# Moving the output groups of a fused MLP's step behind its third product

## The chip, the cores and the metric

The kernel runs on one core of a Trainium2 chip. The metric is device time in microseconds. Each execution is timed by itself. The profile is one further execution, taken by the hardware profiler.

## What is computed

The program is three layers in a row, all in fp32: an attention with landmarks, a first MLP with a SiLU, and a second, gated MLP, which the change touches. Cut to that one:

```python
def _moe2_ref(x, w_gate, w_val, w_out, rms_g):     # x is 2304 x 512, d_ff 1536
    rms = np.sqrt(np.mean(x * x, axis=-1, keepdims=True) + 1e-06)
    xn = x / rms * rms_g
    g = xn @ w_gate
    silu = g * (1.0 / (1.0 + np.exp(-g)))
    val = xn @ w_val
    return (silu * val @ w_out).astype(np.float32)
```

## The kernel before

The second MLP takes the 2304 tokens in three passes p of two blocks of 384, and the 1536 hidden channels in twelve tiles f of 128. One pair (p, f) is a step, i = 12 p + f, 36 in all, each made by `moe2_step`. A step needs, for each of its two blocks, a 128 x 384 tile of g and one of val. It forms these four products of matrices by a scheme in the manner of Strassen and Winograd: seven products of half depth (k = 0 to 6) with sums of the weights and of x as operands. A product is six matmuls with 384 columns (line 843): two halves of the depth, and each fp32 operand as a pair of a rounded part and its remainder, of which three of the four combinations are taken.

Products are written to two PSUM banks, x and y (one buffer each, `pg`). Product 0 starts bank x; products 2, 3 and 5 add onto it. Product 1 starts bank y; product 4 starts y anew, and product 6 adds onto it. Between two products on a bank its value is read: after product 0 ScalarE copies x to a1, after product 1 VectorE adds y to a1 (g1) and ScalarE takes its SiLU (z1); after product 2 x is copied to u2, after 3 to u3; after 4 v2 = u3 + y on VectorE; after 5 z2 = SiLU(x) on ScalarE; after 6 v1 = u2 + y on VectorE. Then VectorE multiplies z2 by v2 and z1 by v1, and each result is split: a cast on ScalarE (line 146), the remainder on VectorE (line 147). In the rows the step's number and the digits of names are left out: `a<-ga` is a1, `g<-a,gb` is g1, `u<-ga` is u2 or u3, `v<-u,gc` is v1 or v2, `z<-ga` is z2, `u<-z,v` a gated product and `CAST u<-u` its cast. Helpers record these at line 180. `ga` is bank x, `gb` and `gc` are bank y.

The other six PSUM banks hold the output sums of a pass, one for each 128 tokens. The results of a step are multiplied with w_out in the step after it: `out(n)`, n = 0 to 5, calls `out_tile`, three matmuls with 512 columns (line 917). Groups 0 to 2 use the half that is made from z2, groups 3 to 5 the half made from z1 and v1. At the last tile of a pass the group's bank is copied to SBUF and stored. Between the products `moe2_step` also calls `between(k)`, k = 0 to 6, which issues work for later steps: in steps 7 to 10 `late` makes the weight operands of the next step (sums at line 577, splits by `split_w`, stores at lines 589 and 592); in the first two passes a piece of the next pass's norm (`norm_all`: squares, sums, a mean by TensorE at line 773 with its copy at line 774, roots, scaling), and from tile 9 on the splits of the next pass's x (`split_x`, lines 807 and 808). The mean's two results borrow banks x and y. In step 0 two splits of x are left for `between(0)` and `between(2)`.

The order on each engine is fixed when the program is built. The framework tracks what each instruction needs, and of those that are ready by its reckoning it takes for an engine the one that stands earliest in the program; so work that is ready early can stand far ahead of its place in the code. `tc.issue_after(ins)` keeps an instruction behind another: each output group behind the latest product (`mm[0]`), each piece of the norm behind VectorE's and ScalarE's latest. All loads and stores of this part, but for a few of the last outputs, go through SP's queue; the next weights are loaded by `load_split(i + 2)` (line 628) once product 6 has freed their tile, and the output weights by `load_wo2` (line 637).

Of the kernel before, what the change touches and what calls it, by code (L numbers as in the profile page):

```python
# [67 lines left out]
def nystrom_moe_kernel(ctx: ExitStack, tc: tile.TileContext, q, k, v, w_in, w_out, w_gate, w_val, w_out2, rms_g, out):  # L68
# [75 lines left out]
    def split(dst, src, lo=POOL, hi=ACT):  # L144

        x = ACT.copy(dst[:, 0], src) if hi is ACT else hi.tensor_copy(dst[:, 0], src)  # L146
        return x, lo.tensor_tensor(dst[:, 1], src, dst[:, 0].bitcast(F32), op=ALU.subtract)  # L147
# [36 lines left out]
    def finish(gn):  # L184
        for _ in gn:
            pass
# [377 lines left out]
    NI = NB2 // 2 * NF2  # L564

    def load_f32(f):
        fw_t[f] = p2.tile([P, 3 * DM], F32, tag="fw", name=f"fw_{f}", bufs=2)
        SP.dma_start(out=fw_t[f], in_=w2d[f])
# [55 lines left out]
    def load_split(i):  # L624

        if NI > i > 0 and (i >= NF2 or i in PRE):
            w7_t[i] = w7_tile(i, f"w7_{i}")
            SP.dma_start(out=w7_t[i].rearrange("p x n -> p (x n)").bitcast(F32), in_=w7d[i % NF2])
# [4 lines left out]
    def load_wo2(i):  # L633
        if i < NI and (i >= NF2 or i in PRE):
            if i:
                wo2_t[i] = wo2_tile(i)
            SP.dma_start(out=wo2_t[i].rearrange("p x n -> p (x n)").bitcast(F32), in_=wod[i % NF2])

    def late(i, k):

        if PRE_N <= i < NF2:
            if k == 0:
                w7_t[i] = w7_tile(i, f"w7_{i}")
                wo2_t[i] = ps2.tile([P, 2, DM], F32R, tag="oc", name=f"oc_{i}", bufs=3)
            if k < 2:
                sums(i, 2 * k)
                sums(i, 2 * k + 1)
            if k in (0, 1, 3, 4):
                split_w(i, w7_t[i], k - (k > 2))
            if k in (2, 3, 5, 6):  # L650
                store_w(i, w7_t[i], k - 2 - (k > 4))
            if k == 5:
                split(wo2_t[i], fw_t[i][:, 2 * DM:], lo=DVE)
        if PRE_N < i <= NF2 and k == 0:
            store_wo(i - 1, wo2_t[i - 1])
# [142 lines left out]
    def split_x(p, k):  # L798
        j = 7 * (p % 2) + k
        if j < 12:  # L800
            t = (p3x if j < 5 else p3).tile([P, 2, 2, TB], F32R, tag=f"x{j}", name=f"x7_{p}_{k}", bufs=1)
        else:
            t = p2.tile([P, 4 * TB], F32R, tag="fw", name=f"x7_{p}_{k}", bufs=2).rearrange("p (x i t) -> p x i t", x=2, i=2)
        x7[p, k] = t
        c = nx[p][OPS[k]]
        for i in range(2):
            ACT.copy(blocked(t[:, 0, i]), by_landmark(c[:, i]))
            DVE.tensor_tensor(blocked(t[:, 1, i]), by_landmark(c[:, i]), blocked(t[:, 0, i].bitcast(F32)), op=ALU.subtract)
# [17 lines left out]
    def moe2_step(p, f, prev, between):  # L826


        i = p * NF2 + f
        if PRE_N <= i + 2 < NF2:  # L830
            load_f32(i + 2)
        if i:
            load_wo2(i + 1)
        w7 = w7_t[i].rearrange("p x (o k n) -> p x o k n", o=7, k=2)

        def tmp(name):
            return p3t.tile([P, TB], F32, tag=name, name=f"{name}_{i}", bufs=1 if name in ("a1", "g1", "u3", "v2", "z2") else 2)

        def product(k, acc, start, stop):
            o, xs, n = WAT[OPS[k]], x7[p, k], 0  # L840
            for kk in range(2):
                for (x, y) in ((0, 0), (0, 1), (1, 0)):
                    mm[0] = PE.matmul(acc, w7[:, x, o, kk], xs[:, y, kk], start=start and n == 0, stop=stop and n == 5, skip_group_check=True)  # L843
                    n += 1

        def added(name, x, y):
            t = tmp(name)
            VE.tensor_tensor(t, x, y, op=ALU.add)
            return t

        def gated(j, gate, val):
            u = tmp(f"u{j}")
            VE.tensor_tensor(u, gate, val, op=ALU.mult)
            hl = p3t.tile([P, 2, TB], F32R, tag="hl", name=f"u2_{i}_{j}", bufs=4)
            split(hl, u, lo=DVE)
            return hl

        hls, mm = [None, None], [None]

        def out(n):  # L860
            with tc.issue_after(mm[0].ins):
                out_tile(prev, n)

        def copied(name, x):
            t = tmp(name)
            AE.copy(t, x)
            return t

        def silu(name, x):
            t = tmp(name)  # L870
            AE.activation(t, x, AF.Silu)
            return t

        x, y = pg(f"ga_{i}", "x"), pg(f"gb_{i}", "y")
        product(0, x, True, True)
        a1 = copied("a1", x)
        between(0)
        product(1, y, True, True)
        z1 = silu("z1", added("g1", a1, y))
        between(1)  # L880
        out(0)
        product(2, x, False, True)
        u2 = copied("u2", x)
        between(2)
        out(1)
        out(2)
        product(3, x, False, True)
        u3 = copied("u3", x)
        between(3)
        y = pg(f"gc_{i}", "y")  # L890
        product(4, y, True, True)
        v2 = added("v2", u3, y)
        between(4)
        out(3)
        product(5, x, False, True)
        hls[1] = gated(1, silu("z2", x), v2)
        between(5)
        out(4)
        product(6, y, False, True)
        load_split(i + 2)  # L900
        hls[0] = gated(0, z1, added("v1", u2, y))
        between(6)
        out(5)
        return p, f, hls, wo2_t[i]

    oacc = {}
# [1 line left out]
    def out_tile(prev, n):  # L908

        if prev is None:  # L910
            return
        p, f, hls, w = prev
        j, t = 1 - n // 3, n % 3
        if f == 0:
            oacc[n] = po.tile([P, DM], F32, tag="o", name=f"o_{p}_{n}", bufs=6)
        for i, (x, y) in enumerate(((0, 0), (0, 1), (1, 0))):
            PE.matmul(oacc[n], hls[j][:, x, t * P:(t + 1) * P], w[:, y], start=f == 0 and i == 0, stop=f == NF2 - 1 and i == 2)  # L917
        if f == NF2 - 1:
            e = nslot(n, f"e2_{p}_{n}", [P, DM])
            last = 0 if p < NB2 // 2 - 1 else 1 + n // 5  # L920
            if last < 2:
                (DVE.tensor_copy if n % 2 else ACT.copy)(e, oacc[n])
            else:
                DVE.tensor_copy(e[:, :DM // 2], oacc[n][:, :DM // 2])
                ACT.copy(e[:, DM // 2:], oacc[n][:, DM // 2:])
            store_out(e, (2 * p + j) * 12 + t * 4, last)

    def pg(name, tag):
        return pp.tile([P, TB], F32, tag=tag, name=name, bufs=1)
# [169 lines left out]
    for p in range(NB2 // 2):  # L1099
# [3 lines left out]
        def between(k):  # L1103
            if x0 and k in (0, 2):
                split_x(0, x0.pop(0))
            late(p * NF2 + f + 1, k)
            if nxt:
                if 0 < f < NORM_END:
                    next(jobs[0], None)
                elif f:  # L1110
                    if f == NORM_END and k == 0:
                        finish(jobs[0])
                    n = 7 * (f - NORM_END) + k
                    if n in XSPLIT:
                        split_x(nxt, XSPLIT.index(n))
# [17 lines left out]
        for f in range(NF2):  # L1133
            if nxt and f == 1:
                jobs[0] = norm(nxt)
            prev = moe2_step(p, f, prev, between)
# [38 lines left out]
```

## Time and profile before

| | us |
|---|---|
| median of 3 runs | 847.81 (847.7 to 847.9) |
| the profiled execution | 848.19 |
| its span, first to last instruction | 845.2 |
| TensorE busy in it | 827.2 |

The page gives busy times by engine. The view of stretches gives them for parts of the span, with the clock that TensorE was granted as a share of full speed. The view in order of time merges like instructions that follow each other: the start, the time from the first one's start to the last one's end, the engine, the line, what is written and read, the count, and in brackets how long the engine was idle before it and who ended that.

### The profile page before, as it was taken

The page shows a single profiled execution, that of the slowest core. Times are in us where ns is not written, and L with a number is a line of the kernel's source. Part 1 is how long each engine was busy: PE and PEld are TensorE (multiplying, and loading weights), DVE is VectorE, ACT ScalarE, POOL GpSimd, SP SyncE. Part 2 cuts the span into 40 slices and gives each one's busy share as a digit, 9 for nine tenths or more (in the row PEclk, how much of TensorE's full clock was granted, in tenths as well). Part 3 has the DMA queues.
Part 4 walks back from the last instruction along what each step waited for, and adds up shares of the span by engine and source line. Part 5 has one row for each costly group of instructions (what it writes and reads, how often), then busy time and mean ns, then how long its engine had stood idle before and what let it go on. Part 6 is the DMA issues. An engine that isn't in the chain of part 4 may idle for free.

```text
span 845.2 us, 15430 instructions
## 1 busy us (share of the span) xinstructions
PE 827.2 (98%) x5934; PEld 735.3 (87%) x5934; DVE 534.0 (63%) x1185; ACT 446.8 (53%) x919; POOL 20.3 (2%) x47
## 2 busy tenths in 40 slices
PE   6899999999999999999999999999999999999997
PEld 3567787988898989999999999999999999999996
DVE  5879877786579767679844489733558523333333
ACT  2796665676666856676643457533345423223222
POOL 5100000000000000000000000000000000000001
PEclk9899999999999999999999999999999999999999
DMA  9788757368795569998985548667555458555552
GB/s 307 307 286 303 291 169 225 107 205 259 268 332 175 171 205 353 329 362 290 333 296 189 213 174 275 247 237 301 224 220 191 179 202 292 224 214 186 183 200 75
DMA packets 72424, 202.85 MB, mean 240 GB/s; under 512 B 6592, under 2 KB 34240, under 8 KB 68384
## 3 DMA queue, kind: packets, MB, share of 16 engines
q1 hardware_dynamic: 72032, 201.09, 66.8%
q8 instruction: 47, 0.77, 0.4%
q0 software_dynamic: 240, 0.66, 0.3%
q14 instruction: 25, 0.20, 0.1%
q10 hardware_dynamic: 80, 0.13, 0.0%
HBM read 149.29 MB, written 52.56 MB: 239 GB/s over the span
## 4 chain that ended last, share of the span: by engine, by line
PE 95%; DVE 1%; ACT 1%; DMA 1%; issue 0%; SPq 0%; POOL 0%; POOLq 0%
PE a L694 21%; PE ga L843 18%; PE o L917 18%; PE h L674 13%; PE gc L843 9%; PE gb L843 4%; PE a L691 4%; PE pw L502 2%; PE pe L316 1%; DMA kT<-in_k_dram 1%; PE pu L435 1%; PE c L309 1%; PE pq L309 1%; PE ct L418 1%; PE spare L248 1%
## 5 line engine op out<-in xcount | busy, mean ns | idle before, releaser
L694 PE MATMUL a<-hl,wo 128*128 128x288 f32 x1296 | 192.3, 297 | 0.0
L694 PEld LDWEIGHTS a<-hl,wo 128*128 128x128 f32 x1296 | 178.3, 188 | 1.7 <-issue 0.8
L917 PE MATMUL o<-oc,u 128*128 128x512 f32 x648 | 178.9, 394 | 0.0
L843 PE MATMUL ga<-x,w 128*128 128x384 f32 x840 | 171.1, 338 | 0.0
L843 PEld LDWEIGHTS ga<-x,w 128*128 128x128 f32 x840 | 151.3, 188 | 12.4 <-ACT a L180 0.3
L674 PE MATMUL h<-at,wp 128*128 128x288 f32 x768 | 132.5, 307 | 0.0
L917 PEld LDWEIGHTS o<-oc,u 128*128 128x128 f32 x648 | 119.5, 188 | 13.3 <-DVE u L147 0.3
L674 PEld LDWEIGHTS h<-at,wp 128*128 128x128 f32 x768 | 109.6, 189 | 22.6 <-issue 8.6
L180 DVE TENSOR_TENSOR v<-u,gc 128x384 f32<-128x384 f32 x72 | 39.7, 552 | 122.6 <-PE gc L843 122.0
L843 PE MATMUL gc<-x,w 128*128 128x384 f32 x420 | 84.8, 336 | 0.0
L681 ACT ACTIVATE s<-h 128x288 f32<-128x288 f32 x108 | 44.0, 411 | 69.2 <-PE h L674 60.9
L843 PEld LDWEIGHTS gc<-x,w 128*128 128x128 f32 x420 | 75.0, 188 | 2.9
L180 ACT COPY u<-ga 128x384 f32<-128x384 f32 x72 | 34.5, 479 | 71.7 <-PE ga L843 71.4
L146 ACT CAST u<-u 128x384 fp32r<-128x384 f32 x72 | 37.0, 514 | 61.2 <-DVE u L180 61.1
L180 DVE TENSOR_TENSOR u<-z,v 128x384 f32<-128x384 f32 x72 | 40.1, 557 | 46.1 <-ACT z L180 45.1
L147 DVE TENSOR_TENSOR hl<-s,hl 128x288 fp32r<-128x288 f32 x108 | 49.0, 453 | 29.3 <-ACT hl L146 28.7
L147 DVE TENSOR_TENSOR u<-u,u 128x384 fp32r<-128x384 f32 x72 | 40.0, 556 | 26.3 <-ACT u L146 26.0
L180 ACT ACTIVATE z<-ga 128x384 f32<-128x384 f32 x36 | 17.7, 491 | 68.4 <-PE ga L843 68.2
L146 ACT CAST hl<-s 128x288 fp32r<-128x288 f32 x108 | 46.6, 434 | 2.9
L691 PE MATMUL a<-s,wor 128*128 128x288 f32 x160 | 42.9, 407 | 0.0
L843 PE MATMUL gb<-x,w 128*128 128x384 f32 x210 | 42.4, 336 | 0.0
L843 PEld LDWEIGHTS gb<-x,w 128*128 128x128 f32 x210 | 37.0, 188 | 0.2
(167 smaller groups left out, 938.0 us busy)
## 6 DMA issues: line engine op xcount, KB each, us to landing
w<-w7d SPq DMA_DIRECT2D x31, 1792.0 KB, 7.3
oc<-wod SPq DMA_DIRECT2D x32, 512.0 KB, 7.8
win<-wind SPq DMA_DIRECT2D x20, 512.0 KB, 5.5
w2d<-c SPq DMA_DIRECT2D x36, 256.0 KB, 2.5
fw<-w2d SPq DMA_DIRECT2D x12, 768.0 KB, 6.4
winr<-in_moe_w_in_dram SPq DMA_DIRECT2D x8, 1024.0 KB, 8.4
wor<-in_moe_w_out_dram SPq DMA_DIRECT2D x16, 512.0 KB, 7.4
w7d<-w7p SPq DMA_DIRECT2D x16, 512.0 KB, 5.7
```

The source lines that it names most:

```text
L146: x = ACT.copy(dst[:, 0], src) if hi is ACT else hi.tensor_copy(dst[:, 0], src)
L147: return x, lo.tensor_tensor(dst[:, 1], src, dst[:, 0].bitcast(F32), op=ALU.subtract)
L180: self.last = getattr(self.eng, name)(*args, **kw)
L248: PE.matmul(spare[0], mean_w, mean_w.unsqueeze(1).to_broadcast([P, 4, P]), start=True, stop=True)
L309: x = PE.matmul(out[o], lm[y, i, R], t[y, i, lo:hi], start=True, stop=True)
L502: x = PE.matmul(pw[g][32 * i:32 * i + 32], lts[b][hr, i], win_t[i // 2, nb_][hr, i % 2], start=True, stop=True)
L674: PE.matmul(ph, w[:, x, fo:fo + P], a[:, y, tk], start=i == 0, stop=i == 5)
L681: ACT.activation(s, ph, AF.Silu)
L691: PE.matmul(acc[d], w[:, y], hl, start=start, stop=stop)
L694: PE.matmul(acc[d], w[:, x, y], hl[:, z], start=start and i == 0, stop=stop and i == 2)
L843: mm[0] = PE.matmul(acc, w7[:, x, o, kk], xs[:, y, kk], start=start and n == 0, stop=stop and n == 5, skip_group_check=True)
L917: PE.matmul(oacc[n], hls[j][:, x, t * P:(t + 1) * P], w[:, y], start=f == 0 and i == 0, stop=f == NF2 - 1 and i == 2)
```

## The change

The six output groups of a step, which stood in ones and twos behind products 1, 2, 4, 5 and 6, all stand behind product 2. All seven calls of `between` come behind them, where each stood behind its own product. The products then follow as 3, 4, 5, 6 with nothing between them. In the last step of all one group stays behind product 2, and the other five stand behind product 6. No instruction is added or removed.

```diff
         x, y = pg(f"ga_{i}", "x"), pg(f"gb_{i}", "y")
+        late_out = 1 if i == NI - 1 else 6
         product(0, x, True, True)
         a1 = copied("a1", x)
-        between(0)
         product(1, y, True, True)
         z1 = silu("z1", added("g1", a1, y))
-        between(1)
-        out(0)
         product(2, x, False, True)
         u2 = copied("u2", x)
-        between(2)
-        out(1)
-        out(2)
+        for n in range(late_out):
+            out(n)
+        for k in range(7):
+            between(k)
         product(3, x, False, True)
         u3 = copied("u3", x)
-        between(3)
         y = pg(f"gc_{i}", "y")
         product(4, y, True, True)
         v2 = added("v2", u3, y)
-        between(4)
-        out(3)
         product(5, x, False, True)
         hls[1] = gated(1, silu("z2", x), v2)
-        between(5)
-        out(4)
         product(6, y, False, True)
         load_split(i + 2)
         hls[0] = gated(0, z1, added("v1", u2, y))
-        between(6)
-        out(5)
+        for n in range(late_out, 6):
+            out(n)
         return p, f, hls, wo2_t[i]
```

## Rows read from the trace of the kernel before

**Rows 1.** The page, busy time by engine: us, share of the span, instructions.

```profile
PE 827.2 (98%) x5934; PEld 735.3 (87%) x5934; DVE 534.0 (63%) x1185; ACT 446.8 (53%) x919; POOL 20.3 (2%) x47
```

**Rows 2.** Stretches: length, busy time of each engine, TensorE's granted clock, DMA.

```profile
480.00:520.00 40.00, 40.00 (x209) 37.02 (x208) 31.60 (x62) 24.41 (x46) 0.00 (x0) 1.00 0.57 206
...
720.00:760.00 40.00, 40.00 (x210) 37.24 (x209) 13.35 (x25) 12.06 (x25) 0.00 (x0) 1.00 0.59 225
```

**Rows 3.** In order of time, TensorE in the last step but one.

```profile
812.03 1.20 PE L843 MATMUL ga<-x,w 128*128 128x384 f32 x6
...
814.81 1.22 PE L843 MATMUL ga<-x,w 128*128 128x384 f32 x6
815.87 1.55 PE L917 MATMUL o<-oc,u 128*128 128x512 f32 x6
...
821.81 1.22 PE L843 MATMUL gc<-x,w 128*128 128x384 f32 x6
822.87 0.86 PE L917 MATMUL o<-oc,u 128*128 128x512 f32 x3
823.56 1.21 PE L843 MATMUL ga<-x,w 128*128 128x384 f32 x6
```

**Rows 4.** In order of time, step 0 and the start of step 1.

```profile
422.90 1.20 PE L843 MATMUL ga<-x,w7p 128*128 128x384 f32 x6
...
423.94 0.88 PE L843 MATMUL gc<-x,w7p 128*128 128x384 f32 x4
...
426.05 0.48 ACT L180 COPY u<-ga 128x384 f32<-128x384 f32 x1 [0.41 <-PE ga L843]
...
426.58 1.33 PE L843 MATMUL ga<-x,w7p 128*128 128x384 f32 x6 [0.22 <-ACT u L180]
427.75 1.22 PE L843 MATMUL gc<-x,w7p 128*128 128x384 f32 x6
...
428.81 1.21 PE L843 MATMUL ga<-x,w 128*128 128x384 f32 x6
...
429.01 0.56 DVE L180 TENSOR_TENSOR v<-u,gc 128x384 f32<-128x384 f32 x1
...
429.86 1.20 PE L843 MATMUL gb<-x,w 128*128 128x384 f32 x6
...
430.11 0.48 ACT L180 COPY a<-ga 128x384 f32<-128x384 f32 x1 [0.53 <-PE ga L843]
430.68 0.51 ACT L146 CAST u<-u 128x384 fp32r<-128x384 f32 x1
```

**Rows 5.** In order of time, the mean in bank x, from step 4 into 5.

```profile
472.75 0.49 ACT L180 ACTIVATE z<-ga 128x384 f32<-128x384 f32 x1 [2.32 <-PE ga L843]
...
473.95 0.56 DVE L774 COPY rv<-pm 128x384 f32<-128x384 f32 x1
...
475.51 0.34 PE L843 MATMUL ga<-x,w 128*128 128x384 f32 x1
```

**Rows 6.** In order of time, the start of step 8.

```profile
510.56 1.21 PE L843 MATMUL ga<-x,w 128*128 128x384 f32 x6
...
511.36 1.14 ACT L146 CAST w<-t 128x512 fp32r<-128x512 f32 x2
...
512.81 0.47 ACT L180 COPY a<-ga 128x384 f32<-128x384 f32 x1
...
513.35 1.32 PE L843 MATMUL ga<-x,w 128*128 128x384 f32 x6
```

**Rows 7.** In order of time, ScalarE at the start of the last step.

```profile
824.69 0.51 ACT L146 CAST u<-u 128x384 fp32r<-128x384 f32 x1 [1.68 <-DVE u L180]
825.11 0.47 ACT L180 COPY a<-ga 128x384 f32<-128x384 f32 x1
```

**Rows 8.** In order of time, TensorE's weight loads at the end.

```profile
837.90 1.22 PEld L917 LDWEIGHTS o<-oc,u 128*128 128x128 f32 x6 [0.29 <-DVE u L147]
```

**Rows 9.** DMA issues: what, queue, operation, count, size, median us to landing.

```profile
w<-w7d SPq DMA_DIRECT2D x31, 1792.0 KB, 7.3
```

## The prediction

> **What bounds the kernel now.** The first thing read is the page's busy times: TensorE works in 98% of the span [rows 1]. The second is the table of stretches inside the second MLP, where the change lies: TensorE is busy for all of each stretch at a granted clock of 1.00, while VectorE is busy 31.6 of 40 us in one stretch and 13.4 in another [rows 2]. So this part is bound by TensorE's own columns, and an edit that adds and removes no matmul can gain only what lies between matmuls, and can lose wherever it takes work away from behind which another engine now hides.
>
> The third view is one quiet step in order of time [rows 3]. From one first product to the next it takes 823.56 - 812.03 = 11.53 us. Products 2 and 6 hold TensorE for 1.06 us (814.81 to 815.87, 821.81 to 822.87), an output group for 0.69 (822.87 to 823.56). Seven products and six groups give about 7 x 1.05 + 6 x 0.69 = 11.5, so nothing is idle. The fourth is step 0 with the start of step 1 [rows 4], which has no output groups before it, since there is no previous step: it shows what the products do when they stand directly behind each other, as the change wants them.
>
> **The change, part by part.** Its diff moves output groups and filler work only. Products alternate between two PSUM banks, x (products 0, 2, 3, 5) and y (1, 4, 6). Between two products on a bank an engine has to read it. I call this a turn.
>
> *What a turn needs.* A product's six matmuls show as 1.22 us, but the next product starts 1.05 later, so the last one drains for about 0.17. Product 6 ends at 427.75 + 1.22 = 428.97 and the add that reads it starts at 429.01: 0.04. The add takes 0.56. A ScalarE copy takes 0.48; the one at 426.05 ends at 426.53, and the product that waits for it shows at 426.58, 0.05 later, and lasts 1.33 in place of 1.22, so 0.11 of weight load is uncovered [rows 4]. From a product's end to the next use of its bank this makes 0.04 + 0.48 + 0.05 + 0.11 = 0.68 us behind ScalarE and 0.76 behind VectorE. One product in between gives 1.05 - 0.17 = 0.88. So a turn with a single product in it still has 0.20 to spare with ScalarE and 0.12 with VectorE. Step 0 agrees: product 6 runs at 427.75, product 0 at 428.81 and product 1 at 429.86 without a gap.
>
> *What is taken away.* Today the turns hold, beside a product, one or two output groups of 0.69. After the change the six groups (4.1 us) all lie in the turn of product 2 to 3. Five turns of a step are left with one product: a1 (product 0 to 2), u3 (3 to 5), v2 (4 to 6), z2 (5 to the next 0), v1 (6 to the next 1). The groups' own inputs do not get late: the halves of the previous step are ready before its next product 2 ends, since the cast of the second one stands at 430.68 [rows 4] and the fourth group starts 2.1 us behind the run's start. In a quiet step all five turns fit, so they cost 0; the bounds are 0 and, with 0.1 missing in each, 0.5 a step.
>
> *What may come back.* A product that follows an output group takes 1.06, product 2 of step 0, which follows a product, 1.04 (422.90 to 423.94); products 5 and 6 of step 0 are no cleaner (product 6 takes 427.75 to 428.81, 1.06). Three products a step lose such a neighbour. At best that is 3 x 0.02 x 35 = 2.1 us; I take the one that is clean in step 0 [rows 4], 0.02 x 35 = 0.7, and keep 0 and 2.1.
>
> *The mean of the norm.* In steps 4 and 16 two matmuls of the mean borrow bank x and two bank y (line 773). The pair on x waits for z2, and the next step's product 0 waits for its copy. Today product 6 and an output group lie in between: z2 starts at 472.75, the copy ends at 473.95 + 0.56 = 474.51, product 0 comes at 475.51 [rows 5]. Without that group it would come at 474.81. From z2's start to the copy's end are 1.76 us; with 0.09 ahead (0.04, and the 0.05 of the weight load's signal) and 0.16 behind that is 2.0 after product 5's end, against 1.05 + 0.35 - 0.17 = 1.23 of matmuls: 0.8 uncovered. The pair on y now comes before product 4 is written and is hidden by product 3, which gives back about 0.3. So +0.5 in each of two steps, +1.0; bounds 0 and +1.6.
>
> *The fillers.* The weight splits of late (steps 7 to 10) and the splits of x for the next pass move behind the run. In the program they now stand before products 3 to 6, but each engine's order is fixed by readiness, and they can go ahead of a1 and v1 as soon as their slot is free. The trace shows this today in step 8 [rows 6]: two weight casts, 1.14 together, stand before a1, which could start at 510.56 + 1.21 + 0.04 = 511.81 and starts at 512.81. Product 2 behind it takes 1.32 in place of 1.22, 0.1 lost although a group of 0.69 still lay in the turn. With the group gone the same delay would cost 0.8. But the order is made anew, so I take one cast in front of a1 in each of four steps, 0.57 - 0.20 = 0.37, in all 1.5; and a VectorE subtraction of the add's shape in front of v1 or v2 in three turns, 3 x (0.56 - 0.12) = 1.3. Sum 2.8. The lower bound is 0 (all of it finds its place in the 4.1 us of groups, where both engines have little else to do), the upper one such delay in all five turns of seven busy steps, 7 x 5 x 0.44 = 15.
>
> *Edges and queues.* The last step keeps one group behind product 2 and has five behind product 6: the 0.29 wait near the end [rows 8] goes, of which TensorE's next matmul feels perhaps 0.2; product 3 there has 0.69 - 0.17 = 0.52 for a turn of 0.68, which costs 0.16. Net 0. The load of the next weights (lines 626 to 628) is still issued behind product 6, but the product that needs it comes one group, 0.7, sooner: 11.5 us against 7.3 to landing [rows 9]; hidden, and 0 too. The stores of late now precede that load on SP's queue; they are ready several products earlier, so they hold nothing up. The evictions of steps 12 and 24 fall into the run, where nothing waits for them within a step.
>
> **Sum.** -0.7 + 1.0 + 2.8 + 0 = +3.1 us. The profiled execution took 848.19, 0.38 over the median of 847.81, so the sum is put on the median: about 850.8.
>
> **The rivals.**
> *No difference.* The fillers fit into the run and cost nothing. Then -0.7 + 1.0 = +0.3: 848.1. For it speaks that VectorE has room even in the busy stretch [rows 2]; against it the start of step 8 [rows 6], where casts go far ahead of their place.
>
> *Faster.* Fillers cost 0, and all three products recover 0.02: -2.1 + 0.5 gives 846.2, and with the mean hidden too 845.7. It decides from the point where the turns cost less than 0.4 in all. Against it speaks product 6 of step 0.
>
> *The wrong order on ScalarE.* In quiet steps today the cast of u stands before a1 (824.69, then 825.11 [rows 7]). If that order stayed, a1 would have to wait for v1 (0.04 + 0.56), the product u of the same shape (0.56, and 0.04 to start), the cast's share of 0.42, then 0.48 + 0.16: 2.26 after product 6's end, where product 2 wants 2 x 1.05 - 0.17 = 1.93. That loses 0.3 in each of 34 steps, 10 to 11: 858. Against it: in step 1, where no group lies behind product 6, a1 already goes first (430.11, cast 430.68). The Trainium skill, Perfetto Trace Analysis, section Optimizing Tensor Performance, asks that independent groups of matmuls rotate through different PSUM banks so that reading one out overlaps the next group. It speaks against this change, which runs seven products over two banks where output groups on six others used to lie between; step 0 [rows 4] shows two banks sufficing as long as nothing stands in front of the reader.
>
> **How the numbers follow.** A run tells about 0.2%, 1.7 us, from no change. Forecast (fillers delay a few turns, 849 to 854) 0.48; no difference 0.28; faster 0.12; wrong order or every busy turn paying 0.12. The forecast's low edge adds 0.04 to the middle. So faster 0.12, same 0.32, slower 0.56. The range goes from 846.2 to 857.0: it takes in the faster case's better half and most of the busy-turn bound, and leaves out the full 15.
>
> **What would show it.** Right: quiet steps still at 11.5 us; the idle time of TensorE before products 2, 1 and 6 named after ScalarE's copy and VectorE's adds, in steps 7 to 10 and around 20 only; steps 4 and 16 longer by half a microsecond. Wrong: quiet steps that are longer (the third rival), or shorter than 11.48 (the second), or steps 7 to 10 without idle time (the first).

## The result and the profile after

The changed kernel takes 853.2 us (median of 4 runs, 853.0 to 853.7) against 847.85 (847.7 to 847.9) for the kernel before: ratio 1.0064, 95% interval 1.005 to 1.0078, so it is slower by 5.35 us. The forecast was slower, 850.8, with a range of 846.2 to 857.0. The profiled execution took 853.25, with a span of 850.8 against 845.2.

The page's busy times by engine:

```profile
PE 830.1 (98%) x5934; PEld 733.5 (86%) x5934; DVE 531.7 (62%) x1185; ACT 446.0 (52%) x919; POOL 20.3 (2%) x47
```

The two stretches, with the columns of [rows 2]:

```profile
480.00:520.00 40.00, 39.31 (x197) 34.75 (x196) 29.80 (x58) 23.51 (x45) 0.00 (x0) 1.00 0.57 209
720.00:760.00 40.00, 40.00 (x211) 37.42 (x210) 11.86 (x23) 11.12 (x23) 0.00 (x0) 1.00 0.58 215
```

TensorE's busy time is 2.9 us above that of [rows 1] for the same 5934 matmuls, and its share is the same: this row doesn't tell where the time went. In the busy stretch it was full before and now has 0.69 us idle, and VectorE gets through less work in the same 40 us (29.80 against 31.60). The quiet stretch is as full as it was. The clock stands at 1.00 in both, so it is no part of the story.

A quiet step in order of time, TensorE and one add of VectorE (the counterpart of [rows 3]; output groups are now line 911):

```profile
819.57 1.20 PE L843 MATMUL ga<-x,w 128*128 128x384 f32 x6
820.61 4.34 PE L911 MATMUL o<-oc,u 128*128 128x512 f32 x18
824.79 1.23 PE L843 MATMUL ga<-x,w 128*128 128x384 f32 x6
825.86 1.20 PE L843 MATMUL gc<-x,w 128*128 128x384 f32 x6
826.90 1.22 PE L843 MATMUL ga<-x,w 128*128 128x384 f32 x6
827.16 0.56 DVE L180 TENSOR_TENSOR v<-u,gc 128x384 f32<-128x384 f32 x1 [6.18 <-PE gc L843]
827.96 1.22 PE L843 MATMUL gc<-x,w 128*128 128x384 f32 x6
829.01 1.20 PE L843 MATMUL ga<-x,w 128*128 128x384 f32 x6
...
831.10 1.20 PE L843 MATMUL ga<-x,w 128*128 128x384 f32 x6
```

From one product 2 to the next (819.57 to 831.10) are 11.53 us, exactly as before, with the eighteen matmuls of the groups in one run and seven products back to back. So the loss is not spread over the steps. The table gives the length of each kind of step, from the start of one product 1 to the start of the next, in the two profiles; steps 5 and 6, and 17 and 18, are taken together, since TensorE's order crosses their border.

| | before | after | difference |
|---|---|---|---|
| first product starts at | 420.82 | 421.10 | +0.28 |
| steps 4 and 16 (mean of the norm) | 12.48, 12.53 | 12.97, 13.05 | +1.01 |
| 5 with 6, 17 with 18 | 23.14, 23.18 | 24.41, 24.35 | +2.44 |
| steps 7, 8, 9 | 34.70 | 35.69 | +0.99 |
| steps 19, 20, 21 | 34.71 | 34.96 | +0.25 |
| steps 1, 14, 25 | 34.63 | 35.20 | +0.57 |
| the other 20 whole steps | 11.53 to 11.58, step 0 7.99 | within 0.02 each | -0.1 |
| last step from product 1 on | 20.61 | 20.73 | +0.12 |

Together +5.56, against 5.57 between the spans. What TensorE's weight loads waited for in the second MLP (the four largest; us in total, times, longest) says who is late:

```profile
PEld gb L843 <- DVE v L180: 2.1, 3, 1.0
PEld ga L843 <- ACT u L180: 1.5, 5, 0.5
PEld ga L843 <- DVE rv L774: 1.2, 2, 0.6
PEld ga L843 <- ACT a L180: 1.2, 4, 0.4
```

The third line is the mean. The first, with a wait of 1.0, is the largest, and nothing in the prediction has that size. It lies at the end of step 5. TensorE, ScalarE and VectorE there, in order of time:

```profile
480.06 4.34 PE L911 MATMUL o<-oc,u 128*128 128x512 f32 x18
...
481.12 1.28 ACT L780 ACT_TABLE_LOAD   x1
482.42 0.94 ACT L780 ACTIVATE rv<-rv,eps 128x768 f32<-128x768 f32 x1
...
486.35 1.22 PE L843 MATMUL ga<-x,w 128*128 128x384 f32 x6
...
487.65 1.28 ACT L180 ACT_TABLE_LOAD   x1 [1.61 <-PE ga L843]
...
488.67 0.55 DVE L180 TENSOR_TENSOR v<-u,gc 128x384 f32<-128x384 f32 x1 [1.49 <-PE gc L843]
488.95 0.49 ACT L180 ACTIVATE z<-ga 128x384 f32<-128x384 f32 x1
...
489.27 0.62 PE L843 MATMUL gb<-x,w 128*128 128x384 f32 x2 [0.65 <-DVE v L180]
...
489.73 1.20 PE L843 MATMUL ga<-x,w 128*128 128x384 f32 x6
```

The norm's square root (line 780) is one of the things that `between` issues. With the fillers it moved into the run of groups, where its own table load costs nothing. But the next SiLU (z2, behind product 5) needs its own table back. That load stands right ahead of z2 and, though its row names nothing that it reads, starts only when product 5 is done (486.35 + 1.22 = 487.57): in ScalarE's order the semaphore wait for product 5, which ends at 487.62, stands ahead of the load. So z2 starts at 488.95 instead of about 487.67. Product 0 of the next step, which needs bank x from z2, comes at 489.73; at a quiet step's pace it would have come two products, 2.11, behind product 5, at 488.46. That is 1.27 us. The wait row names v1, since TensorE's order has two matmuls of product 1 ahead of product 0 here; but v1 is prompt (488.67, against product 6's end at 487.41 + 1.22 = 488.63), and it is z2 that product 0 needs. Before, the same two loads stood thus:

```profile
483.00 1.28 ACT L780 ACT_TABLE_LOAD   x1
...
483.99 1.22 PE L843 MATMUL ga<-x,w 128*128 128x384 f32 x6
...
484.30 0.94 ACT L780 ACTIVATE rv<-rv,eps 128x768 f32<-128x768 f32 x1
...
485.05 0.86 PE L917 MATMUL o<-oc,u 128*128 128x512 f32 x3
...
485.29 1.28 ACT L180 ACT_TABLE_LOAD   x1
...
486.59 0.49 ACT L180 ACTIVATE z<-ga 128x384 f32<-128x384 f32 x1
...
486.80 0.86 PE L917 MATMUL o<-oc,u 128*128 128x512 f32 x3
...
487.50 1.21 PE L843 MATMUL ga<-x,w 128*128 128x384 f32 x6
```

z2 was as late behind its product as now (486.59 against the product's end at 485.21, 1.38; after, 488.95 against 487.57), but two output groups of 0.69 lay in that turn, and TensorE felt at most the 0.08 by which step 5 (11.61) was longer than a quiet one. The table load is not new. Its cover went.

### The profile page after: what moved, and what is told of

Same layout as the page of the kernel before. It is cut to its first block, busy times and chain, and to the rows that moved or that the text cites. A ratio compares the mean times of both kernels' runs of the same rounds, so it can differ in the third digit from the quotient of the medians.

```text
span 850.8 us, 15382 instructions
## 1 busy us (share of the span) xinstructions
PE 830.1 (98%) x5934; PEld 733.5 (86%) x5934; DVE 531.7 (62%) x1185; ACT 446.0 (52%) x919; POOL 20.3 (2%) x47
## 4 chain that ended last, share of the span: by engine, by line
PE 90%; ACT 4%; DMA 3%; DVE 2%; issue 1%; SPq 0%; ACTq 0%
PE ga L843 18%; PE a L694 18%; PE o L911 18%; PE h L674 11%; PE gc L843 9%; PE gb L843 5%; PE a L691 4%; PE pw L502 2%; PE pe L316 1%; DMA r_g<-in_moe_w_gate_dram 1%; DMA kT<-in_k_dram 1%; PE pu L435 1%; PE c L309 1%; DMA w7d<-w7p 1%; PE pq L309 1%
## 5 line engine op out<-in xcount | busy, mean ns | idle before, releaser
L911 PE MATMUL o<-oc,u 128*128 128x512 f32 x648 | 156.4, 394 | 0.0
L843 PEld LDWEIGHTS ga<-x,w 128*128 128x128 f32 x840 | 148.7, 188 | 6.3 <-DVE rv L774 1.2
L911 PEld LDWEIGHTS o<-oc,u 128*128 128x128 f32 x648 | 121.5, 188 | 25.5
```

## The experiments

**Which part of the move costs: the groups or the fillers.** First the run of groups alone, with each filler left behind its own product (against the changed kernel):

```diff
         product(0, x, True, True)
         a1 = copied("a1", x)
+        between(0)
         product(1, y, True, True)
         z1 = silu("z1", added("g1", a1, y))
+        between(1)
...
         for n in range(late_out):
             out(n)
-        for k in range(7):
-            between(k)
+        between(2)
```

and so on for 3 to 6.

> Only the output groups are moved; the seven calls of between stand behind their own products again. Theory (the loss lies in other engines' work that falls into turns with one product): the pieces of the norm now fall right into these turns, a square root with its table loads behind u3 among them, so it is slower than the changed kernel, 854 to 858 us, with long waits in steps 5 and 17 and more of them in steps 6 to 8 and 18 to 20. Rival (the loss comes from the moved fillers, not from the groups): 848 to 849 us.

Measured: 856.2 (855.96 to 856.85), ratio to the kernel before 1.01 (1.0085 to 1.0114): 3 us worse than the change as it is. Steps 4 and 16 grow to 14.2 each, 2.4 of the 3; steps 7 to 9 do not get longer (35.44). So taking the fillers into the run does pay, and above all in the two steps of the mean.

Then the reverse, the fillers behind product 2 and the groups at their old places:

```diff
+        out(0)
         product(2, x, False, True)
         u2 = copied("u2", x)
-        for n in range(late_out):
-            out(n)
+        out(1)
+        out(2)
         for k in range(7):
             between(k)
...
         u3 = copied("u3", x)
...
+        out(3)
```

with groups 4 and 5 behind products 5 and 6.

> Only the calls of between are moved behind product 2; the output groups stand where they stood before. Theory: every turn keeps its 0.69 or more of groups, so the square root, the table loads and the casts are hidden as before: 847.3 to 848.6 us, no difference. Rival (the moved fillers are what costs): 851 to 853 us.

Measured: 847.12, ratio 0.999 (0.9982 to 0.9999). Moving the fillers alone costs nothing; the 0.08 to 0.11 that steps 5 and 8 had lost before are gone (11.53 each). The whole loss needs the groups out of the turns.

**The table of the SiLU.** If the reload ahead of z2 is the cause, it must vanish when something calls for that table at once, while the run of groups covers the load. A SiLU of one column, whose result nobody uses, follows the square root:

```diff
+    touch = cst.tile([P, 9], F32, name="touch")[:, 0:1]
...
+        if p:
+            ACT.activation(touch, rv[:, 1, TB - 1:], AF.Silu)
```

> The changed kernel with one more ScalarE instruction behind the norm's square root: a SiLU of one column, whose result is not used, so that the table of the SiLU comes back while the output groups run. Theory: product 0 behind steps 5 and 17 waits for z2 because of a table load of 1.28 us in front of it; both steps get shorter by about 1.2, the time falls by 2.4 us to about 850.8. Rival (VectorE's reciprocals hold up v1 and v2 in these steps): no fall, 853.

Measured: 847.4 (846.2 to 849.6), ratio 0.9993 (0.9985 to 1.0002). Steps 5 with 6 fell to 22.86, but the time fell by more than expected, since the quiet steps fell too, to 11.43 to 11.46, and they hold no square root. The new tile of nine columns moves the tiles allocated behind it. So the experiment was made anew with nothing moved: the result goes to a column of a tile that was there already and was unused.

```diff
-    eps = cst.tile([P, 9], F32, name="eps")[:, 0:1]
+    eps9 = cst.tile([P, 9], F32, name="eps")
+    eps, touch = eps9[:, 0:1], eps9[:, 8:9]
...
+        if p:
+            ACT.activation(touch, rv[:, 1, TB - 1:], AF.Silu)
```

> The changed kernel with the SiLU of one column behind the square root, written into a column that the kernel before already holds unused, so that nothing moves in SBUF. Theory: quiet steps stay at 11.53, steps 5 and 6 together fall from 24.4 to 23.1 us, as do 17 and 18: 850.7. Rival (all that the first form of this won was the place of the tiles): 853.2.

Measured: 850.06 (849.4 to 850.6), ratio 1.0025 (1.0015 to 1.0035). ScalarE in step 5, in order of time:

```profile
480.95 1.28 ACT L781 ACT_TABLE_LOAD   x1
482.25 0.94 ACT L781 ACTIVATE rv<-rv,eps 128x768 f32<-128x768 f32 x1
483.20 1.28 ACT L783 ACT_TABLE_LOAD   x1
...
487.44 0.49 ACT L181 ACTIVATE z<-ga 128x384 f32<-128x384 f32 x1 [1.62 <-PE ga L846]
```

The reload stands in the run and z2 has none ahead of it. Steps 5 with 6 take 23.06 and 17 with 18 take 23.14, no more than before the change; the quiet steps stay at 11.53. That is 2.56 us less in these four steps, of the 3.1 by which the time fell; the rest lies in steps 7 and 25 (0.3 together) and in the last step.

The Trainium skill, ScalarE: Activation LUTs, section What ACT_TABLE_LOAD costs, gives 1283 ns for the load and 1380 ns of draining for every switch. The rows agree with the first and not with the second: the SiLU of z2 starts 0.02 us behind its load's end, and the load 0.05 behind the square root's end in the kernel before.

**The place of the tiles.** To see what a moved tile does by itself, the same nine unused columns were put into the kernel before, and into the changed kernel:

```diff
     eps = cst.tile([P, 9], F32, name="eps")[:, 0:1]
+    pad = cst.tile([P, 9], F32, name="pad")[:, 0:1]
+    POOL.memset(pad, 0.0)
```

The kernel before with it:

> The kernel before with one small tile more (nine columns, of which one is set to 0 and none is read), which moves every later tile in SBUF; no instruction of the step changes. Theory (the hundredths that separate 1.04 from 1.06 us of a product hang on where the operands lie, as the SiLU of one column suggested, whose own tile moved them too): quiet steps of 11.41 to 11.46 in place of 11.53 to 11.57, 35 x 0.1 = 3.5 us less, 844 to 845. Rival (they come from output groups next to products): quiet steps as before, 847.9.

The changed kernel with it:

> The changed kernel with the same unused tile. Theory: quiet steps of 11.41 to 11.46, the waits of steps 4 to 8 and 16 to 20 unchanged: 849.5 to 850. Rival: 853.2.

Measured: 846.79, ratio 0.999 (0.9981 to 0.9999), and 849.68, ratio 1.0023 (1.0014 to 1.0032). Quiet steps take 11.51 (11.48 between 12 and 22) in the first and 11.43 to 11.46 (11.41) in the second. The first missed what was expected: the tiles' place alone gives 0.02 to 0.09 a step. The rest comes with the run of groups, and only in this layout. TensorE in a quiet step of the changed kernel with the nine columns:

```profile
805.95 4.28 PE L913 MATMUL o<-oc,u 128*128 128x512 f32 x18
810.07 1.23 PE L845 MATMUL ga<-x,w 128*128 128x384 f32 x6
...
812.18 1.20 PE L845 MATMUL ga<-x,w 128*128 128x384 f32 x6
813.21 1.20 PE L845 MATMUL gc<-x,w 128*128 128x384 f32 x6
```

The run takes 4.12 where it took 4.18, product 5 takes 1.03 where it took 1.06. Why the same matmuls are faster with their tiles elsewhere stays open.

**The mean of the norm.** In steps 4 and 16 alone, the fillers stand ahead of the run and both blocks' means use bank y, which leaves bank x to product 0:

```diff
-            pm = psum(f"pm_{p}_{j}", [P, TB]) if p == 0 else pg(f"pm_{p}_{j}", "xy"[j])
+            pm = psum(f"pm_{p}_{j}", [P, TB]) if p == 0 else pg(f"pm_{p}_{j}", "y")
...
+        mean_step = i in (4, NF2 + 4)
+        if mean_step:
+            for k in range(7):
+                between(k)
...
-        for k in range(7):
-            between(k)
+        if not mean_step:
+            for k in range(7):
+                between(k)
```

> The changed kernel, but in steps 4 and 16 the calls of between stand ahead of the six groups, and both means of the norm borrow bank y. Theory: bank x is no longer borrowed between z2 and the next product 0; steps 4 and 16 fall from 13.0 to 12.2 us (11.53 and four matmuls of 0.17), the time by 1.5 us or a little less, to about 851.8. Rival (the four matmuls themselves and their order make up the length): steps of 12.9 or more, 853.

Measured: 851.98, ratio 1.0045 (1.0033 to 1.0057). Steps 4 and 16 take 12.54 each: 0.9 of the 1.0 that they had lost, though 12.2 was expected. The wait is gone from product 0; about 0.3 a step stays, where the weight loads of the mean now wait for VectorE (0.8 us in two waits). Two things were changed at once, the bank and the place of the fillers. That the wait of product 0 for the mean's copy (1.2 us in two waits) is gone speaks for the bank; neither was changed alone.

**How much a turn has to spare.** One more copy of bank x by ScalarE, ahead of u3, in steps 25 to 35, first in the changed kernel, then in the kernel before. It repeats work already done.

```diff
         product(3, x, False, True)
+        if i > 2 * NF2:
+            copied("a1", x)
         u3 = copied("u3", x)
```

> The changed kernel, with one more ScalarE copy of bank x ahead of u3 in the last eleven steps (25 to 35). The copy repeats work, the outputs stay. In the changed kernel u3's turn (product 3, 4, 5) holds one product alone. The prediction worked out 0.68 us needed and 0.88 there, 0.20 to spare. The second copy delays u3 by 0.37 (two neighbouring copies start so far apart) to 0.43. Theory (0.20 to spare): each of these steps gets longer by 0.17 to 0.23, from 11.53 to about 11.73, 1.9 to 2.5 us in all, TensorE waiting ahead of product 5. Rival 1 (no spare time, any delay goes straight to TensorE): 0.37 or more per step, 11.90, over 4 us. Rival 2 (far more spare than worked out): 11.53 to 11.60.

> The same extra copy ahead of u3 in the kernel before, in steps 25 to 35. There one output group of 0.69 lies beside product 4 in that turn, so a delay of 0.4 stays hidden: steps 11.53 as before, the time within 0.5 us of the kernel before. Rival (ScalarE's further work is late by it): up to 0.1 per step, 1 us.

Measured, one execution each: 854.46 and 848.02. In the changed kernel steps 26 to 34 take 11.76 each, 0.23 more; in the kernel before they stay at 11.53. (The time itself rose by only 1.2, because in this execution the first product came 1.4 us sooner; the steps show it cleanly.) One of these turns in the changed kernel with the copy, in order of time:

```profile
791.56 0.48 ACT L180 COPY a<-ga 128x384 f32<-128x384 f32 x1 [4.40 <-PE ga L843]
791.93 0.49 ACT L180 COPY u<-ga 128x384 f32<-128x384 f32 x1
792.47 1.00 PEld L843 LDWEIGHTS ga<-x,w 128*128 128x128 f32 x6 [0.29 <-ACT u L180]
```

u3 is late by 791.93 - 791.56 = 0.37 and TensorE by 0.23, so the turn had 0.14 to spare. That is less than the 0.20 worked out, but neither rival holds: the spare time is not zero, and not so large that nothing was felt. With the groups in their old places the same delay was free.

**Single late starts.** Steps 1, 14 and 25 lost 0.13 to 0.30 each though no filler stands in their turns. Three places in the changed kernel, in order of time:

```profile
437.46 1.20 PE L843 MATMUL gc<-x,w 128*128 128x384 f32 x6
...
439.12 0.55 DVE L180 TENSOR_TENSOR v<-u,gc 128x384 f32<-128x384 f32 x1 [6.59 <-PE gc L843]
439.73 1.00 PEld L843 LDWEIGHTS gc<-x,w 128*128 128x128 f32 x6 [0.33 <-DVE v L180]
...
592.19 0.48 ACT L180 COPY u<-ga 128x384 f32<-128x384 f32 x1 [3.20 <-PE ga L843]
...
715.18 0.48 ACT L180 COPY a<-ga 128x384 f32<-128x384 f32 x1 [0.74 <-PE ga L843]
```

In the first, product 4 ends at 438.66 and VectorE starts 0.46 later, where a quiet step has 0.10 (825.86 + 1.20 = 827.06, 827.16). Nothing stood ahead of it. Counting every instruction of an engine, semaphore waits too, the wait right ahead of VectorE's two late adds (this one and v2 of step 8) is its 959th and its 1087th, 128 apart. In the kernel before, the adds at the same two places are late too, at 436.76 and 518.62, where groups in the turn hid them. ScalarE's late starts stand behind its 831st, 959th and 1087th (z2 of step 7 and the two rows above). To shift ScalarE's stream by itself, it got six copies of one column in step 0, into the spare column of a tile:

```diff
         product(2, x, False, True)
         u2 = copied("u2", x)
+        if not i:
+            with tc.issue_after(AE.last.ins):
+                for _ in range(6):
+                    ACT.copy(touch, eps)
         for n in range(late_out):
             out(n)
```

> The changed kernel with six more copies of one column on ScalarE in step 0, written to a spare column of a tile that is there already, so no tile moves; the outputs stay. Theory (single late starts sit at fixed places of an engine's own instruction stream, 128 instructions apart, and the run of groups merely uncovers them): ScalarE's late starts fall on instructions six places earlier in the work, so steps 14 and 25 go from 11.70 and 11.67 back to 11.57 and 11.53 unless the new place is also the head of a turn; VectorE's stream is untouched, so steps 1 and 8 stay at 11.83. Rival (late starts come with the work of these steps): all four stay. The time changes by less than 0.5 us either way.

Measured: 852.72 in one execution. Steps 14 and 25 fall from 11.70 and 11.67 to 11.58 and 11.53, and step 7 from 12.06 to 11.93. Steps 1 and 8 stay (11.81, 11.85). The copy a1 at the same place as the last row above, in this kernel:

```profile
713.65 1.20 PE L844 MATMUL ga<-x,w 128*128 128x384 f32 x6
...
714.95 0.48 ACT L181 COPY a<-ga 128x384 f32<-128x384 f32 x1 [0.46 <-PE ga L844]
```

It starts 0.10 behind its product's end (714.85) instead of 0.38. So these starts belong to a place in the engine's stream and not to the step.

**A version that beats both.** The fillers behind product 2 and the groups at their old places (the second experiment) with the nine unused columns:

> The output groups where they stood before, only the calls of between behind product 2, and the unused tile: the candidate that should beat both kernels. Theory: 847.1 less 3.5, so 843.6, and faster than the kernel before by 0.4 to 0.5%. Rival: 847.

Measured: 846.47 (845.9 to 847.4), ratio 0.9984 (0.9975 to 0.9992): faster than both kernels, though far from the 843.6 expected, for the same reason as the kernel before with the columns: without the run its quiet steps stay at 11.51. So the last one mixes the two orders by step:

```diff
+        apart = 4 <= i <= 10 or 16 <= i <= 21
...
+        if apart:
+            out(0)
         product(2, x, False, True)
         u2 = copied("u2", x)
-        for n in range(late_out):
+        for n in (1, 2) if apart else range(late_out):
             out(n)
...
+        if apart:
+            out(3)
```

> Put together from what the runs showed: the unused tile of nine columns as in the padded kernels, the fillers behind product 2 in all steps, the output groups at their old places in steps 4 to 10 and 16 to 21, in a run behind product 2 in the others. If the run of groups gains 0.07 to 0.08 per quiet step in this layout (11.51 against 11.43), then about 22 quiet steps give 1.7: 844.7 against 846.5 of the padded kernel with the groups at their old places, and 847.9 of the kernel before, faster than both. Rival (the gain does not come where steps of both orders alternate, or is given back by late starts at the heads of turns): 846 to 847.

Measured: 845.89 (844.75 to 847.26) with the kernel before at 848.33 on that chip, ratio 0.9976 (0.9967 to 0.9985). It is the fastest of all by its ratio, but above the 844.7 expected and nearer to the rival. Its interval overlaps the one of the padded kernel without the run, and its 35 steps are no shorter (400.89 against 400.73; the kernel before 402.75). The run did give its 0.08 in quiet steps (11.43). Steps 4 and 16 gave 0.7 back (12.75 and 12.78 against 12.41 and 12.40), and steps 1, 15, 22 and 25 together 0.5, three of them by a late start at the head of a turn. The gain of mixing is not shown; that of the columns with the moved fillers is.

## Why the prediction was right, and where it was not

The sign, the size to 2.4 us and most of the places were right. More than half of the loss came from two things that the sum did not hold. That the time still fell well inside the range is in part luck: the fillers were priced 2.0 too high, and what the sum lacked came to 3.7. (The sum itself is 847.81 + 3.1 = 850.9; 850.8 is a slip of 0.1.)

**The turns.** That quiet steps would stay at 11.5 was right, to the hundredth. The 0.20 and 0.12 to spare were each 0.06 too large. ScalarE's is 0.14 by the extra copy. VectorE's is about 0.06: its start at 439.12 was late by 0.36 and step 1 lost 0.30. The part mis-sized is the 0.04 from a product's end to its reader [rows 4], which in quiet steps is 0.10 for a1, u3, v2 and z2; only v1, which follows other work of VectorE, keeps 0.04 (829.22, against 827.96 + 1.22 = 829.18). The Trainium skill's rule that independent groups of matmuls should rotate through different PSUM banks (Perfetto Trace Analysis, Optimizing Tensor Performance) spoke against the change and pointed the right way. In these rows two banks sufficed while every reader was prompt (11.53), and a reader late by 0.37 cost TensorE 0.23.

**What may come back, -0.7.** It was 0. Product 2 did fall from 1.06 to 1.04 and product 6 from 1.06 to 1.05, but the groups take 4.18 in one run, where six of them in ones and twos took 4.16, and product 3 and 5 keep 1.07 and 1.06. That the tiles' place decides whether the run gains was not thought of.

**The mean, +1.0.** Measured +1.01, in the two steps named, and by the wait named:

```profile
475.57 0.61 PE L773 MATMUL pm<-sh,mean_w 128*128 128x384 f32 x2
...
476.22 0.56 DVE L774 COPY rv<-pm 128x384 f32<-128x384 f32 x1
...
476.83 1.31 PE L843 MATMUL ga<-x,w 128*128 128x384 f32 x6 [0.30 <-DVE rv L774]
```

Product 0 starts 0.05 behind the copy's end; before it came a whole microsecond behind it [rows 5]. The experiment with both means on bank y took 0.9 of this back.

**The fillers, +2.8.** Steps 7 to 9 and 19 to 21 lost 1.24 against before. Of that 0.13 is a late start that the shifted stream took away, and about 0.30 VectorE's in step 8, put at what it cost in step 1; some 0.8 is left for the fillers. The two mechanisms are the ones priced, in the turns named:

```profile
502.24 0.92 ACT L146 CAST w<-fw 128x384 fp32r<-128x384 f32 x2
...
503.07 0.47 ACT L180 COPY a<-ga 128x384 f32<-128x384 f32 x1
...
503.59 1.01 PEld L843 LDWEIGHTS ga<-x,w 128*128 128x128 f32 x6 [0.29 <-ACT a L180]
...
525.69 0.55 DVE L180 TENSOR_TENSOR v<-u,gc 128x384 f32<-128x384 f32 x1
...
526.29 1.01 PEld L843 LDWEIGHTS gb<-x,w 128*128 128x128 f32 x6 [0.19 <-DVE v L180]
```

Two casts stand before a1 in step 7, as [rows 6] had shown for step 8, and at 525.69 v1 comes late behind VectorE's other work. But the run takes in most fillers, so that fewer turns pay than the seven assumed in full.

**Edges and queues, 0.** Measured +0.12, which is not told from 0: with the same order in the last step, other runs here took from 20.35 to 20.85 for it. The wait at the end [rows 8] is gone, and one of 0.3 for u2, ahead of product 3 of the last step, stands in its place, as the turn of 0.52 against 0.68 said.

**What the sum lacked.** The step that failed is the one on what `between` carries. It priced the mean, the splits of the weights and of x, and passed over the square root in step 5 and 17, with its two table loads; the rows at 483.00 to 486.59 were there to be read. So the sign that waits would lie in steps 7 to 10 and around 20 only did not hold: the largest lie at the end of steps 5 and 17. It cost 2.44, shown by the column of SiLU that took it away. The single late starts cost some 1.0 (0.30 in step 1, an estimated 0.30 in 8, 0.13, 0.13 and 0.14 in 7, 14 and 25); two of them were in the trace of before, hidden under groups. The first product's 0.28 lies ahead of the change: other kernels here, with nothing changed before it, had it between 419.7 and 423.1. Together 0 + 1.0 + 0.8 + 0.1 from the terms of the sum and 2.4 + 1.0 + 0.3 outside it make the 5.6.

The wrong order on ScalarE did not come: in the quiet steps a1 stands first (830.31 in the last step) and the cast of u behind it (830.94).

## What to carry to other kernels

An instruction group that sits between two uses of a PSUM bank is cover; before it is moved away, list everything that any step of the loop issues inside that interval, rare steps too, and price each at its full delay. An activation that needs another table is priced with the reload that follows it (1.28 us here), and in this kernel the reload was paid where the next activation stood, however idle the engine was in between; one dummy activation at the idle place moved it there. And a comparison of two orders is safe only with the tiles at the same addresses; check a step that the experiment doesn't touch.

## What was not expected of the hardware

At the five places named above, 128 instructions apart in their streams, ScalarE and VectorE start one instruction late, by 0.26 to 0.28 (ScalarE) and 0.36 us (VectorE) more than the usual 0.10, and each time one packet of about 8 KB on the queue for instructions falls within the same 2.5 us. For the copy at 592.19 (product 3 ends at 590.61 + 1.22 = 591.83), the view of the queues from 591.5 to 594 (packets, MB, share of 16 engines' time):

```profile
q14 instruction: 1, 0.01, 0.8%
```

The page counts 25 such packets in the whole span. In the trace each of the five packets starts 0.7 to 1.2 us behind the late instruction (592.86 for this one), so its arrival is not what that instruction waited for. Whether the fetch of instructions makes the start late stays open. And the same matmuls with nine unused columns ahead of their tiles ran 0.02 to 0.16 us per step faster, by an amount that depends on their order; what it is in the addresses stays open.
